# The last 128 rows of wq for ten heads of each round, laid on partitions 0 to 63 and loaded as eight shares of four rows

## The chip, the cores and the metric

One Trainium2 chip, one core, one launch. The metric is the device time of that launch in microseconds (us). The kernel before took 713.16 us (median of three runs, 712.34 to 713.28).

## The reference

Decoding of one token for a batch of four, through two equal rounds; each round is an attention block and a dense block, each with a residual sum. All arrays are float32.

```
W = 1024                      # the last 1024 of 4096 cached positions; 32 heads of 128; D = 640; Dff = 1728
q = (layernorm(x) @ wq) by heads;  k, v = the last W positions of the caches
p = softmax(q . k * 128**-0.5);  o = p . v
x = x + o @ wo                                   # attention
x = x + relu(layernorm(x) @ w1) @ w2             # dense
# both lines twice, with the same weights and caches
```

For one head this reads 640 x 128 numbers of wq, 4 x 1024 x 128 of k, as many of v, and 128 x 640 of wo: 4.85 MB. The two rounds together read 301 MB from HBM, and there is little arithmetic on each number.

## The kernel before

**The tape.** The host lays everything that belongs to one head side by side as a record of REC = 9472 columns on 128 partitions: columns 0 to 639 are wq (five blocks of 128 rows, each with 128 columns of the head), then 4096 columns of k, 4096 of v and 640 of wo. The 32 records lie one behind the other in `rec`. One partition's row of the tape is contiguous, so a load of n columns is 128 rows of 4n bytes.

**Loads.** `store` holds five records and the front of a sixth, `ring` 4320 columns more. A list `items` is written when the program is built: every load in its order, with its place in `store`, `ring` or `kept`. `pump` (line 278) takes loads from the front of that list as long as the columns they go to are free, and `done` (line 300) frees columns when their last reader has been written down. All loads are issued by SP, in the list's order; an issue waits on the chip until the last reader of its columns is through. `group` (line 210) loads five records as three transfers of some 8 MB (lists FIVE, LAST_FIVE and THREE, lines 82 to 85), `ending` cuts the last three heads finer, and the weights of the dense block (`wm`) follow.

**Work on a head.** `query` (line 385) multiplies x by the head's wq: five matmuls of 128 x 128 with four moving columns, accumulated in `misc`. `scores` makes q . k, `softmax` and `weights` the probabilities, `values` the product with v, `project` the product with wo. Engines run in the order in which the code is written (`InOrder`, line 88): head n+1's scores stand ahead of head n's values on TensorE, and head n+2's query behind them.

**Rounds.** Round 0 takes heads 0 to 31, round 1 heads 27 to 31 first, which are still in `store`, and then 0 to 26. Around the dense block of round 0 the loads are small, as `store` holds the five heads that are kept, and `ring` and what is spare carry the weights and then the front of the next heads.

Of the kernel before, what the change touches and what calls it, by code (L numbers as in the profile page):

```python
# [32 lines left out]
F32 = mybir.dt.float32  # L33
# [5 lines left out]
P = 128  # L39
B, D, H, DH, W, FF = 4, 640, 32, 128, 1024, 1728  # L40
NB = 4
FD = D // NB
KB = FD // 32
# [3 lines left out]
WQ, K, V, WO = 0, D, D + 4 * W, D + 8 * W  # L47
REC = 2 * D + 8 * W
HALF = REC // 2
VH = 2 * W  # L50

NS = 5
# [23 lines left out]
CUTS = [*range(0, K, DH), *range(K, WO, 512), *range(WO, REC + 1, FD)]  # L76
# [2 lines left out]
LATE = 6  # L79


FIVE = [REC + 6272, 2 * REC - 3072, 2 * REC - 3200]
LAST_FIVE = [REC + 4736, 2 * REC - 4736, REC, REC]
THREE = [REC + HALF, REC + HALF]
GROUPS = [{h: FIVE for h in range(0, 25, 5)}, {6: THREE, 9: FIVE, 14: FIVE, 19: LAST_FIVE}]


class InOrder:
# [18 lines left out]


@with_exitstack
def decode_kernel(ctx: ExitStack, tc: tile.TileContext, xf, rec, wm, out):  # L110
# [18 lines left out]
    rows = sb.tile([P, 2 * B], F32, name="rows")  # L129
    pick, rrow = rows[:, :B], rows[:, B:]  # L130
    mrt = sb.tile([P, B], F32, name="mrt")
    small = sb.tile([P, 14], F32, name="small")
# [41 lines left out]
    LAST = H - NS  # L174


    def home(h, r):

        if r:
            return FIRST + (h if h >= LAST else h - 6 + LAST) % NS * REC  # L180
        return (0 if h < NS else FIRST) + h % NS * REC

    items = []

    at = {("rec", 1, LAST - 1): [(KEPT, REC, "kept", 0)], ("rec", 1, 0): [(0, FIRST, "store", 0)]}
    live = []
    spare = home(H - 1, 0)
    buffers = {"store": store, "ring": ring, "kept": kept}

    def load(src, lo, hi, buf, col, parts):  # L190
        items.append((src[:, lo:hi], buf, col, hi - lo, parts))

    def place(buf, col):
        return ("store", spare + FROM + col) if buf == "spare" else (buf, col)
# [1 line left out]
    def weight(r, lo, hi, buf, col):  # L196
        buf, col = place(buf, col)
        load(wm, lo, hi, buf, col, [(("w", r), lo, hi, col)])


    def run(r, lo, hi, buf, col):
        parts = [(("rec", r, h), max(lo - h * REC, 0), min(hi - h * REC, REC), col + max(h * REC - lo, 0))
                 for h in range(lo // REC, (hi - 1) // REC + 1)]
        load(rec, lo, hi, buf, col, parts)

    def piece(r, h, lo, hi, buf="store", col=None):
        run(r, h * REC + lo, h * REC + hi, buf, home(h, r) + lo if col is None else col)


    def group(r, h, sizes):  # L210
        lo = 0
        for size in sizes:
            run(r, h * REC + lo, h * REC + lo + size, "store", home(h, r) + lo)
            lo += size

    def ending(r, hs, late):
        a, b, c = hs[-3:]
# [14 lines left out]
    for h in hs[:-3]:  # L232
        if h in GROUPS[0]:
            group(0, h, GROUPS[0][h])
        if h >= 25:
# [10 lines left out]
    new = hs[NS:]  # L246
# [8 lines left out]
    cuts = [h * REC + x for h in new[1:6] for x in CUTS]  # L255
    c, end = new[1] * REC, new[6] * REC
    for buf, lo, hi in places:
        if lo == old[1]:
            piece(1, new[0], WO, REC, buf, lo)
        elif c < end:  # L260
            cut = max(x for x in cuts if x <= min(end, c + hi - lo))
            run(1, c, cut, buf, lo)
            c = cut
    assert c == end
    for h in new[6:-3]:
        if h in GROUPS[1]:
            group(1, h, GROUPS[1][h])
        if not any(g <= h < g + sum(z) // REC for g, z in GROUPS[1].items()):
            piece(1, h, 0, REC)
    ending(1, hs, False)  # L270
    for ks in W1_SLOT:
# [1 line left out]
    n = 0  # L273
# [4 lines left out]
    def pump():  # L278

        while items:  # L280
            src, buf, col, n, parts = items[0]
# [11 lines left out]
    def cols(key, lo, n):  # L293

        for x, y, buf, col in pieces(key):
            if x <= lo and lo + n <= y:
                return buffers[buf][:, col + lo - x:col + lo - x + n]
# [84 lines left out]
    def xblock(k):  # L382
        return xT[:, 32 * k:32 * k + B]

    def query(r, h, n, first=False):
        key = ("rec", r, h)
        early = r == 1 and n < 2
        q = acc[:, 504 + 4 * n:508 + 4 * n] if early else misc[:, :B]
        for k in range(KB):
            pe.matmul(q, cols(key, WQ + k * DH, DH), xblock(k), start=(k == 0 and not early),  # L390
                      stop=(k == KB - 1), skip_group_check=True)
        done(key, WQ, K)
        if first:
            dve.tensor_copy(qT, q)
        else:
            dve.tensor_tensor(qT, q, rrow, op=OP.mult)
# [104 lines left out]
    for r in range(2):  # L501
        hs = order[r]
        late = LATE if r == 0 else 2
        center(384 * r, 128)
        query(r, hs[0], 0, True)
        if r:
            busy(192, warm)
        scores(r, hs[0], 0, True)
        softmax(0, (r, hs[1], 1))
        if r:  # L510
            unpark(2)
            unpark(3)
# [91 lines left out]
```

## Time and profile before

| what | value |
|---|---|
| three runs | 712.34, 713.16, 713.28 us |
| span of the profiled execution, first to last instruction | 710.7 us |
| HBM read over that span | 301.34 MB, 424 GB/s |
| TensorE matmul busy | 502.4 us (71%) |
| VectorE busy | 317.4 us (45%) |
| ScalarE busy | 99.6 us (14%) |
| largest wait of SP, whose waits are for room in the buffers: PE acc | 355.7 us, 33 times |

The page gives the span of the profiled execution and no time of its own beside it; what lies between the span and the median of the runs is 2.5 us. The busy shares are of the span. A DMA share is a mean over the 16 DMA engines of the core: 0.50 in a window can mean that all sixteen worked half of the time, or that eight of them had finished. Packets are counted in the window in which they start, so in a window of a microsecond or two a share can stand a little over 1.00.

### The profile page before, as it was taken

Reading aid. Unit: us, or ns where it says so; the run is one execution under the profiler, and the core shown is the slowest. Engines: PE = TensorE matmul, PEld = TensorE weight load, DVE = VectorE, ACT = ScalarE, POOL = GpSimd, SP = SyncE. Lnnn points to the kernel's source line nnn. Section 1 sums busy time; section 2 is a strip of 40 time slices with the busy share of each in tenths; the row PEclk is TensorE's granted clock in tenths of the full one; section 3 lists DMA queues with packets and bytes.
Section 4 is the critical chain, followed back from the end, with each engine's and each line's share of the span. In section 5 each row is a group of like instructions: output and inputs, shape, how many; then the busy total and the mean of one; then the engine's idle time right before and its main releaser. Section 6 shows DMA issues by size and latency. Waiting matters only on the chain.

```text
span 710.7 us, 8613 instructions
## 1 busy us (share of the span) xinstructions
PE 502.4 (71%) x3722; PEld 199.5 (28%) x3722; DVE 317.4 (45%) x645; ACT 99.6 (14%) x210; POOL 1.1 (0%) x9
## 2 busy tenths in 40 slices
PE   0675677576677686868788998756577685695985
PEld 0331322231332222333223333322222231332322
DVE  2252344253443353546541866625244253453661
ACT  0210111011010110111130421201010011011120
POOL 0000000000000000000000000000000000000000
PEclk9987787677676778788999999969687677788899
DMA  9999999999999999999999999999999999999996
GB/s 397 436 416 451 422 435 447 417 435 447 420 429 451 427 429 420 425 444 420 426 404 396 411 425 434 447 429 436 442 431 433 434 428 436 430 427 421 430 427 281
DMA packets 12741, 301.97 MB, mean 425 GB/s; under 512 B 1424, under 2 KB 1568, under 8 KB 4640
## 3 DMA queue, kind: packets, MB, share of 16 engines
q1 hardware_dynamic: 12672, 301.42, 98.9%
q8 instruction: 29, 0.48, 0.2%
q14 instruction: 8, 0.07, 0.0%
q10 hardware_dynamic: 32, 0.01, 0.0%
HBM read 301.34 MB, written 0.08 MB: 424 GB/s over the span
## 4 chain that ended last, share of the span: by engine, by line
DMA 68%; PE 25%; DVE 4%; another core or an unknown queue 1%; ACT 1%; issue 1%; SPq 0%; ACTq 0%
DMA store<-rec 60%; PE sc_ps L102 10%; PE o_ps L102 7%; DMA store<-wm 5%; PE acc L102 3%; PE misc L102 3%; DMA ring<-wm 3%; DVE scratch L102 2%; DVE o_ps L102 2%; PE t_ps L102 2%; ACT oTs L102 1%; DVE small L102 0%; ACT sc_ps L102 0%; DVE sc_ps L102 0%
## 5 line engine op out<-in xcount | busy, mean ns | idle before, releaser
L102 PE MATMUL sc_ps<-store,qT 128*4 128x512 f32 x1024 | 193.7, 852 | 37.8 <-DMA store<-rec 36.4
L102 PE MATMUL misc<-xT,store 128*128 128x4 f32 x620 | 92.8, 276 | 100.6 <-DMA store<-rec 100.0
L102 DVE TENSOR_REDUCE small<-sc_ps 128x1 f32<-128x1024 f32 x64 | 78.4, 1224 | 157.9 <-PE sc_ps L102 157.8
L102 PE MATMUL o_ps<-store,scratch 128*16 128x512 f32 x960 | 142.1, 667 | 4.6 <-DVE scratch L102 2.9
L102 PEld LDWEIGHTS misc<-xT,store 128*128 128x128 f32 x620 | 87.4, 221 | 156.2 <-DMA store<-rec 123.1
L102 ACT ACTIVATE sc_ps<-sc_ps,small 128x1024 f32<-128x1024 f32 x64 | 69.8, 1091 | 325.2 <-DVE small L102 325.2
L102 DVE STREAM_TRANSPOSE sc_ps<-sc_ps 128x1024 f32<-128x1024 f32 (+1 forms) x70 | 81.7, 1167 | 0.1
L102 PEld LDWEIGHTS sc_ps<-store,qT 128*4 128x4 f32 x1024 | 32.7, 107 | 121.2 <-issue 66.4
L102 PEld LDWEIGHTS o_ps<-store,scratch 128*16 128x16 f32 x960 | 32.3, 114 | 118.6 <-issue 100.7
L102 DVE TENSOR_TENSOR o_ps<-o_ps,of_block 128x512 f32<-128x512 f32 x62 | 43.4, 699 | 45.9 <-PE o_ps L102 45.8
L102 DVE TENSOR_TENSOR qT<-misc,rows 128x4 f32<-128x4 f32 x61 | 9.5, 156 | 112.7 <-PE misc L102 112.6
L102 PE MATMUL acc<-store,oTs 128*4 128x160 f32 x488 | 34.6, 365 | 17.1 <-ACT oTs L102 17.0
L102 DVE TENSOR_REDUCE scratch<-o_ps 128x128 f32<-128x512 f32 x62 | 42.9, 692 | 2.1
L102 ACT COPY oTs<-t_ps 128x4 f32<-128x4 f32 x59 | 9.6, 162 | 204.5 <-PE t_ps L102 204.5
L102 PE MATMUL t_ps<-rows,scratch 128*128 128x4 f32 x118 | 25.5, 286 | 11.4 <-DVE scratch L102 10.9
L102 PEld LDWEIGHTS t_ps<-rows,scratch 128*128 128x128 f32 x118 | 21.4, 226 | 17.9 <-DVE scratch L102 14.2
L102 DVE TENSOR_TENSOR scratch<-sc_ps,mrt 128x128 f32<-128x128 f32 (+1 forms) x70 | 19.6, 280 | 2.7
L102 PE MATMUL acc<-kept,small 128*1 128x328 f32 (+2 forms) x54 | 17.4, 428 | 0.0
L99 PE MATMUL acc<-scratch,ring 128*128 128x160 f32 x2 | 0.9, 540 | 22.2 <-DMA scratch<-xf 22.2
L102 DVE TENSOR_SCALAR mrt<-of_batch,small 128x4 f32<-128x4 f32 x64 | 14.7, 230 | 2.2
L102 DVE STREAM_TRANSPOSE scratch<-small 128x32 f32<-128x32 f32 x64 | 12.9, 202 | 2.4 <-ACT sc_ps L102 2.4
L102 PEld LDWEIGHTS acc<-store,oTs 128*4 128x4 f32 x488 | 6.9, 84 | 22.9 <-ACT oTs L102 21.9
(84 smaller groups left out, 123.1 us busy)
## 6 DMA issues: line engine op xcount, KB each, us to landing
store<-rec SPq DMA_DIRECT2D x14, 7872.0 KB, 28.9
store<-rec SPq DMA_DIRECT2D x7, 7936.0 KB, 30.9
store<-rec SPq DMA_DIRECT2D x4, 7104.0 KB
store<-rec SPq DMA_DIRECT2D x11, 2368.0 KB, 34.8
store<-rec SPq DMA_DIRECT2D x3, 4736.0 KB, 27.2
store<-rec SPq DMA_DIRECT2D x2, 4416.0 KB, 28.3
store<-rec SPq DMA_DIRECT2D x5, 1024.0 KB, 20.2
store<-rec SPq DMA_DIRECT2D x1, 4160.0 KB, 20.7
```

The source lines that it names most:

```text
L99: r = build(*args, **kwargs)
L102: r = build(*args, **kwargs)
```

## The change

Heads 14 to 23 of each round are "split" (SPLIT). Their records on the tape lose the 128 columns of wq's fifth block (columns 512 to 639), so `rec` is 1280 columns shorter. Those blocks go into a new input, `halves`: for each of the ten heads the block's 128 rows are laid on 64 partitions, rows 0 to 63 in 128 columns and rows 64 to 127 in the 128 columns beside them, 2560 columns in all. In HBM the 64 rows lie as two times eight shares of four rows, with a fifth row of nothing behind each share. In each round two transfers, one to partitions 0 to 31 and one to partitions 32 to 63, bring them to columns 128 to 2687 of `ring`; they stand in the list ahead of the group of head 10 (round 0) and of head 14 (round 1).

The query of a split head is four matmuls as before and then two of 64 rows, the second against `upper`, a copy of the lower half of x's fifth block on partitions 0 to 63. ScalarE makes that copy once a round, at the sixth head of the loop. The sizes in FIVE, LAST_FIVE and THREE are now written as (head, column) of each cut, at the same places.

```diff
+SPLIT = range(14, 24)
+FULL = (KB - 1) * DH
+HALVES = len(SPLIT) * 2 * DH
+HALVES_AT = 128
+HALVES_BEFORE = [10, 14]
+def size(h):
+    return REC - DH if h in SPLIT else REC
...
+    def halves_of(r):
+        parts = [(("halves", r), 0, HALVES, HALVES_AT)]
+        items.append(([(halves[q][:, :4, :HALVES], 32 * q, 32) for q in range(2)], "ring", HALVES_AT, HALVES, parts))
...
+    def group(r, h, cuts):
+        if h == HALVES_BEFORE[r]:
+            halves_of(r)
...
-            sp.dma_start(buffers[buf][:, col:col + n], src)
+            for src, row, rows in shares:
+                sp.dma_start(buffers[buf][row:row + rows, col:col + n], src)
...
-        for k in range(KB):
+        split = h in SPLIT
+        for k in range(KB - split):
             pe.matmul(q, cols(key, WQ + k * DH, DH), xblock(k), start=(k == 0 and not early),
                       stop=(k == KB - 1), skip_group_check=True)
+        if split:
+            c = (h - SPLIT[0]) * 2 * DH
+            pe.matmul(q, cols(("halves", r), c, DH, 64), xblock(KB - 1)[:64], start=False, stop=False,
+                      skip_group_check=True)
+            pe.matmul(q, cols(("halves", r), c + DH, DH, 64), upper, start=False, stop=True, skip_group_check=True)
+            done(("halves", r), c, c + 2 * DH)
...
+            if n == NS:
+                act.copy(upper, xblock(KB - 1)[64:])
...
+    halves = np.zeros((2, 8, 5, HALVES), k.dtype)
...
+            both = np.concatenate([rec[h, :64, a:b], rec[h, 64:, a:b]], 1)
+            halves[:, :, :4, c:c + 2 * DH] = both.reshape(2, 8, 4, 2 * DH)
```

SP's loads of round 0 before the change, from the second on (`store<-rec 128x15744` is a transfer of 128 rows of 15744 columns; three transfers make a group of five heads):

```order
L102 DMA store<-rec 128x15872
L102 DMA store<-rec 128x15744 x2
L102 DMA store<-rec 128x15872
L102 DMA store<-rec 128x15744 x2
L102 DMA store<-rec 128x15872
L102 DMA store<-rec 128x15744 x2
L102 DMA store<-rec 128x15872
L102 DMA store<-rec 128x15744 x2
```

The same loads now, from the same one on, as far as the group of heads 15 to 19:

```order
L132 DMA store<-rec 128x15872
L132 DMA store<-rec 128x15744 x2
L132 DMA store<-rec 128x15872
L132 DMA store<-rec 128x15744
L132 DMA ring<-halves 32x1x2560 x2
L132 DMA store<-rec 128x15744
L132 DMA store<-rec 128x15872
L132 DMA store<-rec 128x15616
L132 DMA store<-rec 128x15488
L132 DMA store<-rec 128x15616 x2
```

Two transfers of 32 rows stand ahead of the group of head 10, and from that group's last transfer on each one is shorter by 128 columns for every split head in it. In round 1 the same pair stands behind the three loads of heads 9 to 13.

TensorE before, where the query of head 14 of round 0 stands among the scores, values and products of its neighbours:

```order
L102 MATMUL sc_ps_74<-store,qT 4x512 x8
L102 MATMUL o_ps<-store,scratch 16x512 x8
L102 MATMUL misc<-xT,store 128x4 x5
L102 MATMUL t_ps<-rows,scratch 128x4
L102 MATMUL acc<-store,oTs 4x160 x4
```

TensorE now, at that head:

```order
L132 MATMUL sc_ps_75<-store,qT 4x512 x8
L132 MATMUL o_ps<-store,scratch 16x512 x8
L132 MATMUL misc<-xT,store 128x4 x4
L132 MATMUL misc<-xT,ring 128x4
L132 MATMUL misc<-upper,ring 128x4
L132 MATMUL t_ps<-rows,scratch 128x4
L132 MATMUL acc<-store,oTs 4x160 x4
```

The query of a split head reads `ring` as well as `store` and has six matmuls where there were five; nothing else changed its place on TensorE.

More of the change, by code (lines that the diff above doesn't have):

```diff
@@ L79, with on_tape, runs_of @@
 LATE = 6
-FIVE = [REC + 6272, 2 * REC - 3072, 2 * REC - 3200]
-LAST_FIVE = [REC + 4736, 2 * REC - 4736, REC, REC]
-THREE = [REC + HALF, REC + HALF]
+FIVE = [(1, 6272), (3, 3200), (5, 0)]
+LAST_FIVE = [(1, 4736), (3, 0), (4, 0), (5, 0)]
+THREE = [(1, HALF), (3, 0)]
 GROUPS = [{h: FIVE for h in range(0, 25, 5)}, {6: THREE, 9: FIVE, 14: FIVE, 19: LAST_FIVE}]
+SPLIT = range(14, 24)
[5 more added lines that the diff above has]
+    return REC - DH if h in SPLIT else REC
+BASE = [sum(size(g) for g in range(h)) for h in range(H + 1)]
+def on_tape(h, lo):
+    return BASE[h] + (lo - DH if h in SPLIT and lo >= K else lo)
+def runs_of(lo, hi):
+    found = []
+    for h in range(H):
+        for a, b in ((0, FULL), (K, REC)) if h in SPLIT else ((0, REC),):
+            at = on_tape(h, a)
+            x, y = max(lo, at), min(hi, at + b - a)
+            if x < y:
+                found.append((h, a + x - at, a + y - at, x - lo))
+    return found
 class InOrder:
@@ L109, in decode_kernel @@
 @with_exitstack
-def decode_kernel(ctx: ExitStack, tc: tile.TileContext, xf, rec, wm, out):
+def decode_kernel(ctx: ExitStack, tc: tile.TileContext, xf, rec, halves, wm, out):
     nc = tc.nc
@@ L131, in decode_kernel @@
     mrt = sb.tile([P, B], F32, name="mrt")
+    upper = sb.tile([64, B], F32, name="upper")
     small = sb.tile([P, 14], F32, name="small")
@@ L174, in decode_kernel, with start @@
     LAST = H - NS
-    def home(h, r):
+    def start(h, r):
         if r:
@@ L181, in home @@
         return (0 if h < NS else FIRST) + h % NS * REC
+    def home(h, r):
+        for g, cuts in GROUPS[r].items():
+            if g and g <= h < g + cuts[-1][0]:
+                return start(g, r) + BASE[h] - BASE[g]
+        return start(h, r)
     items = []
@@ L201, in run @@
     def run(r, lo, hi, buf, col):
-        parts = [(("rec", r, h), max(lo - h * REC, 0), min(hi - h * REC, REC), col + max(h * REC - lo, 0))
-                 for h in range(lo // REC, (hi - 1) // REC + 1)]
-        load(rec, lo, hi, buf, col, parts)
+        load(rec, lo, hi, buf, col, [(("rec", r, h), a, b, col + at) for h, a, b, at in runs_of(lo, hi)])
     def piece(r, h, lo, hi, buf="store", col=None):
[L207 to L214, printed above, removed]
+        assert h not in SPLIT
+        run(r, BASE[h] + lo, BASE[h] + hi, buf, home(h, r) + lo if col is None else col)
+    def group(r, h, cuts):
+        if h == HALVES_BEFORE[r]:
+            halves_of(r)
+        lo = BASE[h]
+        for n, at in cuts:
+            hi = on_tape(h + n, at)
+            run(r, lo, hi, "store", home(h, r) + lo - BASE[h])
+            lo = hi
     def ending(r, hs, late):
@@ L254, in decode_kernel @@
     places += [("store", 0, FIRST), ("store", old[4] + FROM, old[4] + REC), ("ring", 0, RING)]
-    cuts = [h * REC + x for h in new[1:6] for x in CUTS]
-    c, end = new[1] * REC, new[6] * REC
+    cuts = [BASE[h] + x for h in new[1:6] for x in CUTS]
+    c, end = BASE[new[1]], BASE[new[6]]
     for buf, lo, hi in places:
@@ L267, in decode_kernel @@
             group(1, h, GROUPS[1][h])
-        if not any(g <= h < g + sum(z) // REC for g, z in GROUPS[1].items()):
+        if not any(g <= h < g + z[-1][0] for g, z in GROUPS[1].items()):
             piece(1, h, 0, REC)
@@ L280, in pump @@
         while items:
-            src, buf, col, n, parts = items[0]
+            shares, buf, col, n, parts = items[0]
             if any(b == buf and x < col + n and col < y for b, x, y in live):
                 return
-            sp.dma_start(buffers[buf][:, col:col + n], src)
+            for src, row, rows in shares:
+                sp.dma_start(buffers[buf][row:row + rows, col:col + n], src)
             live.append((buf, col, col + n))
@@ L291, in pieces, with cols @@
         return at[key if key in at else (key[0], 0) + key[2:]]
-    def cols(key, lo, n):
+    def cols(key, lo, n, rows=P):
         for x, y, buf, col in pieces(key):
             if x <= lo and lo + n <= y:
-                return buffers[buf][:, col + lo - x:col + lo - x + n]
+                return buffers[buf][:rows, col + lo - x:col + lo - x + n]
         raise KeyError((key, lo, n))
@@ L581 @@
     rec = np.empty((H, P, REC), k.dtype)
+    flat = np.empty((P, BASE[H]), k.dtype)
+    halves = np.zeros((2, 8, 5, HALVES), k.dtype)
     rec[:, :, WQ:K] = block_rows(np.asarray(A_wq)).reshape(KB, P, H, DH).transpose(2, 1, 0, 3).reshape(H, P, D)
@@ L585 @@
     rec[:, :, WO:] = np.asarray(A_wo).reshape(H, DH, D)
+    for h in range(H):
+        a, b = (FULL, K) if h in SPLIT else (K, K)
+        flat[:, BASE[h]:BASE[h + 1]] = np.concatenate([rec[h, :, :a], rec[h, :, b:]], 1)
+        if h in SPLIT:
+            c = (h - SPLIT[0]) * 2 * DH
+            both = np.concatenate([rec[h, :64, a:b], rec[h, 64:, a:b]], 1)
+            halves[:, :, :4, c:c + 2 * DH] = both.reshape(2, 8, 4, 2 * DH)
     w2 = np.asarray(B_w2)
@@ L591 @@
         "xf": x.reshape(B, NB, FD).transpose(1, 0, 2).reshape(NB * B, FD),
-        "rec": rec.transpose(1, 0, 2).reshape(P, H * REC),
+        "rec": flat,
+        "halves": halves,
         "wm": np.concatenate([block_rows(np.asarray(B_w1)).transpose(1, 0, 2).reshape(P, KB * FF), *tiles], 1),
```

2 lines of the change are left out of this document (1 added, 1 removed).

## The prediction

> **What bounds the kernel now.** I read the page's slices, queues and chain first.
>
> ```profile
> span 710.7 us, 8613 instructions
> PE 502.4 (71%) x3722; PEld 199.5 (28%) x3722; DVE 317.4 (45%) x645; ACT 99.6 (14%) x210; POOL 1.1 (0%) x9
> DMA  9999999999999999999999999999999999999996
> q1 hardware_dynamic: 12672, 301.42, 98.9%
> q8 instruction: 29, 0.48, 0.2%
> q14 instruction: 8, 0.07, 0.0%
> DMA 68%; PE 25%; DVE 4%; another core or an unknown queue 1%; ACT 1%; issue 1%; SPq 0%; ACTq 0%
> ```
>
> The DMA engines are busy from the first slice to the last, SP's queue alone fills 98.9% of them, and 68% of the chain that ended last is loads. The kernel is as long as its loads. Two small queues share the engines with it: 29 packets that fetch instructions on q8 and 8 on q14.
>
> The change neither adds nor saves bytes. [...] So the question is whether the sixteen engines end together. No view numbers them, but the last microseconds, in windows of half a microsecond, show how many still work (last two columns: mean share of the sixteen, GB/s):
>
> ```profile
> 702.00:702.50 0.50, 0.50 (x24) 0.42 (x14) 0.00 (x0) 0.00 (x0) 0.00 (x0) 1.00 0.98 410
> 702.50:703.00 0.50, 0.48 (x12) 0.10 (x2) 0.00 (x0) 0.00 (x0) 0.00 (x0) 1.00 0.91 379
> 703.00:703.50 0.50, 0.00 (x0) 0.00 (x0) 0.00 (x0) 0.00 (x0) 0.00 (x0) 1.00 0.74 307
> 703.50:704.00 0.50, 0.00 (x0) 0.00 (x0) 0.00 (x0) 0.00 (x0) 0.00 (x0) 1.00 0.64 261
> 704.00:704.50 0.50, 0.00 (x0) 0.00 (x0) 0.00 (x0) 0.00 (x0) 0.00 (x0) 1.00 0.54 220
> 704.50:705.00 0.50, 0.13 (x4) 0.11 (x8) 0.00 (x0) 0.00 (x0) 0.00 (x0) 1.00 0.39 159
> 705.00:705.50 0.50, 0.50 (x20) 0.40 (x16) 0.00 (x0) 0.00 (x0) 0.00 (x0) 1.00 0.42 169
> 705.50:706.00 0.50, 0.50 (x24) 0.39 (x20) 0.00 (x0) 0.00 (x0) 0.00 (x0) 1.00 0.42 140
> 706.00:706.50 0.50, 0.50 (x19) 0.35 (x14) 0.00 (x0) 0.00 (x0) 0.00 (x0) 1.00 0.17 67
> 706.50:707.00 0.50, 0.50 (x20) 0.34 (x10) 0.00 (x0) 0.00 (x0) 0.00 (x0) 1.00 0.04 15
> ```
>
> Sixteen times the share is the number at work: 15.7, 14.6, 11.8, 10.2, 8.6, 6.2, 6.7, 6.7, 2.7, 0.6. Nine engines end between 702.5 and 704.7, none in the next half microsecond, and the other seven between some 705.3 and 706.8. The half-microseconds times the shares add up to 2.6, so the mean engine ends at 704.6 and the last 2.2 us later. Perfect balance behind the last point at which all wait could gain 2.2 us there, no more.
>
> What delays the late ones? All carry the same rows of the tape, so the fetches do. A window of one microsecond around one fetch of each kind gives its time as a share of sixteen engines; the windows 405 to 707 us and 0 to 355 us give their numbers:
>
> ```profile
> q8 instruction: 1, 0.02, 5.8%
> q14 instruction: 1, 0.01, 1.9%
> ...
> q8 instruction: 14, 0.23, 0.3%
> q14 instruction: 3, 0.02, 0.0%
> ...
> q8 instruction: 12, 0.20, 0.2%
> q14 instruction: 3, 0.02, 0.0%
> ```
>
> A q8 fetch takes 0.058 x 16 = 0.93 us, a q14 fetch 0.30 us. Spread over all sixteen, 14 fetches from 405 us on would set engines apart by one fetch at most. Two clusters with middles 2.5 us apart (703.6 and 706.1) say that they fall on half the engines: 14 on eight is 1.75 each, which asks 1.4 us a fetch, 0.93 and some 0.5 lost beside it by the interrupted packet (an estimate). By the same half microsecond a q14 fetch costs 0.3 to 0.8.
>
> **The change part by part.** *Bytes.* From 560 to 600 us the engines run undisturbed:
>
> ```profile
> 560.00:600.00 40.00, 27.61 (x190) 11.44 (x194) 16.19 (x33) 4.26 (x10) 0.00 (x0) 0.76 1.00 435
> ```
>
> 435 / 16 = 27.2 GB/s an engine. The tape loses 10 heads x 128 columns x 4 bytes = 5,120 bytes on each of 128 partitions a round; an engine that serves eight of them is relieved of 40,960 bytes, 1.51 us. The new transfers bring eight shares of four rows of 10,240 bytes, twice: 81,920 bytes on each of eight engines, 3.01 us (at the 25.1 GB/s an engine of the window 705.0 to 705.5, where rows are 5 KB and less, 3.26). So in each round eight engines get 1.5 to 1.75 us more, I take 1.55, and eight get 1.51 less. [...]
>
> [...] No row of before has such a transfer; were all sixteen used, the sum of this part would be nothing.
>
> *Who is late.* If only relieved engines were late, they would end at 706.8 - 2 x 1.51 = 703.8 and the loaded ones, all among the early nine, at 704.7 + 1.55 to 3.1 = 706.3 to 707.8: from 0.5 us better to 1.0 worse, as the move is larger than the gap. But seven are late and nine early, so with eight in a half at least one of the half with the q8 fetches is early, and for each further one an engine of the other half is late. [...] One engine that takes two of the three q14 fetches behind 405 us is 0.6 to 1.6 us behind its neighbours, and from 703.6 that reaches the gap. I take it that one loaded engine ends at 705.3, the early edge of the late cluster.
>
> *What carries from round 0 to the end.* Between the rounds the loads are small and wait for room:
>
> ```profile
> 355.00:405.00 50.00, 42.08 (x410) 15.42 (x406) 22.96 (x58) 12.12 (x23) 0.00 (x0) 1.00 1.01 401
> ...
> 325.79 33.97 DMA store<-rec
> 359.77 8.88 DMA ring<-wm
> ...
> 369.66 6.76 DMA ring<-wm
> ```
>
> 401 GB/s against 435 over 50 us is 3.9 us of lost transfer a mean engine, some of it small rows (at 25.1 GB/s, 402, all of it). So between nothing and 3.9 us of waiting lies here, and early engines wait longest. But each of these loads is waited for until its last engine has landed, and the next is issued after that: a laggard drags the lull with it. So of the 1.55 us that the loaded laggard gets in round 0, between 0 and 1.55 reaches the end; I take 1.4, near the upper end, because the chain is made of load waits until here and so follows the last engine. It ends at 705.3 + 1.4 + 1.55 = 708.25, **1.4 us** behind the 706.8 of now.
>
> *TensorE.* Each split head gets one matmul and one weight load more, and two of the six have 64 rows.
>
> ```profile
> L102 PE MATMUL misc<-xT,store 128*128 128x4 f32 x620 | 92.8, 276 | 100.6 <-DMA store<-rec 100.0 <-DVE xT L102 0.3
> PE misc L102 <- DMA store<-rec: 21.8, 5, 6.4
> PE misc L102 <- DMA store<-rec: 20.7, 5, 6.5
> ```
>
> A matmul of a query is two instructions (620 = 2 x 310), so at most 0.55 us a head and 5.5 us for the ten heads of a round. The cover is in TensorE's waits from 150 to 270 us and from 530 to 660 us, which hold the split heads of the two rounds: it waits for loads ahead of queries 21.8 and 20.7 us, five times each. It costs nothing. Without that cover it would be 5.5 us a round. The 64-row form is not in the trace; between nothing and a full matmul it hides the same way.
>
> *ScalarE's copy.* The nearest row is the 128 x 4 copy:
>
> ```profile
> 439.59 0.16 ACT L102 COPY oTs<-t_ps 128x4 f32<-128x4 f32 x1 [1.21 <-PE t_ps L102]
> ```
>
> 0.16 us twice, ahead of an exponential for which ScalarE waits anyway (1.21 us idle before this copy). Nothing, or 0.3 us if that idle time were gone.
>
> *SP.* Two issues more a round, at some 0.35 us each, ahead of an issue that waits for room; the columns of `ring` they fill were left by the opening or by head 5 long before. No new wait falls on what stands behind them. [...]
>
> **Sum.** 0 (TensorE, ScalarE, SP) + 1.4: the span goes from 710.7 to 712.1 us. The profiled execution lies 2.5 us under the median of the runs, which I keep: **714.6 us**.
>
> **The rivals.**
>
> *The late half is the relieved half and no loaded engine is late.* For it speak the two clusters. As above, the lull eats much of round 0's share: 706.3 to 706.6, so 712.5 to 713.0, take 712.7. Chance 0.22.
>
> *Faster.* The same, and the lull eats all of round 0's load on the early engines while the relieved ones keep both of theirs; the last loaded engine that matters is then one near the middle of the early cluster, 703.6 + 1.55 = 705.2, and the gain is 1.6 us: 711.5. It decides from the point where the laggards of the stretch up to 360 us are all relieved ones, as then the lull itself comes up to 1.5 us earlier, too. Against it: q14's fetches. Chance 0.16.
>
> *The late half is the loaded half.* Then both loads fall on the last engine: 2 x 1.5 to 1.75, 716.2 to 716.7. Nothing in the views excludes it, since none numbers the engines. Chance 0.07.
>
> *The relieved engines stand idle while the shares load.* The 2 x 327,680 bytes of a round last 3.0 us on eight engines instead of 1.5 on sixteen; if the next 8 MB transfer doesn't follow at once on the other eight, every round loses 1.5 us: 713.2 + 3.0 = 716.2. It decides where the next issue comes later than the shares' end. Against it stand the full slices: the queue always holds a transfer more. Chance 0.05. [...]
>
> *The shares do not do what they say* and go over all sixteen engines: only some 16 packets more, 713.2. Chance 0.03.
>
> **How the numbers follow.** The forecast has the rest, 0.47; with all of the laggard's first load kept it is 714.8, with none 713.2. A measurement here can tell about 0.2%, 1.4 us, from no change, and the forecast lies on that bound; I put 0.33 of it beyond and 0.14 within. Slower: 0.33 + 0.07 + 0.05 = 0.45. Within: 0.14 + 0.22 + 0.03 = 0.39. Faster: 0.16. The range leaves out the far half of the faster case and what lies beyond the two cases at 716.2: 711.6 to 716.2.
>
> **What would show it.** In the last windows the stair should lose its two clusters: more engines early (the relieved at 702 to 705), and a thin tail of one or two (share 0.06 to 0.12) up to 708. SP's queue should show two transfers of 320 KB to `ring` a round, TensorE's waits under the query should shrink by about 0.5 us a head, and the lull should begin 0 to 1 us later. I am wrong if the last engine ends by 705.5 (no loaded laggard), or if the tail is eight engines wide (the loaded half was the late one).

## The result, and the profile after

The changed kernel takes **718.32 us** (median of six runs, 716.64 to 719.59) against 712.76 for the kernel before beside it: a ratio of 1.0076, 95% interval 1.006 to 1.0092, or 5.4 us slower (4.3 to 6.6). The forecast was 714.6 with a range up to 716.2: the sign was right, the time lies outside.

The page of the changed kernel, the lines that answer to those of before (span; TensorE's busy time; the DMA engines' share in 40 slices; packets, MB and share of time of each queue; the chain that ended last):

```profile
span 716.9 us, 8704 instructions
PE 503.7 (70%) x3762; PEld 208.5 (29%) x3762; DVE 318.5 (44%) x645; ACT 99.9 (14%) x212; POOL 1.1 (0%) x9
DMA  9999999999999999999999999999999999999995
q1 hardware_dynamic: 12832, 301.42, 98.5%
q8 instruction: 29, 0.48, 0.3%
q14 instruction: 8, 0.07, 0.0%
DMA 73%; PE 22%; DVE 2%; ACT 1%; issue 1%; SPq 0%; ACTq 0%
```

The bytes are those of before, the queue is nearly as full as before, and yet it is later. 98.5% of 716.9 us is 706.1 us of packet time an engine, against 98.9% of 710.7, 702.9, before. So about half of the 6.2 us is engines that stand idle at some time, and the other half is the same bytes moved in more time.

Where the engines end, by windows of a microsecond (last two columns: share of the sixteen, GB/s):

```profile
705.00:706.00 1.00, 0.71 (x4) 0.08 (x1) 0.93 (x4) 0.00 (x0) 0.00 (x0) 1.00 1.00 417
706.00:707.00 1.00, 0.00 (x0) 0.00 (x0) 0.22 (x2) 0.00 (x0) 0.00 (x0) 1.00 0.82 339
707.00:708.00 1.00, 0.58 (x20) 0.51 (x24) 0.00 (x0) 0.00 (x0) 0.00 (x0) 1.00 0.78 320
708.00:709.00 1.00, 1.00 (x34) 0.71 (x24) 0.00 (x0) 0.00 (x0) 0.00 (x0) 1.00 0.67 252
709.00:710.00 1.00, 0.22 (x4) 0.00 (x0) 0.00 (x0) 0.00 (x0) 0.00 (x0) 1.00 0.25 102
710.00:711.00 1.00, 0.00 (x0) 0.00 (x0) 0.00 (x0) 0.00 (x0) 0.00 (x0) 1.00 0.15 61
711.00:712.00 1.00, 0.82 (x25) 0.64 (x29) 0.00 (x0) 0.00 (x0) 0.00 (x0) 1.00 0.10 38
712.00:713.00 1.00, 1.00 (x36) 0.74 (x28) 0.00 (x0) 0.00 (x0) 0.00 (x0) 1.00 0.07 26
```

The shares from 705 on add up to 3.8, so the mean engine ends at 708.8, where it was 704.6; the last one ends near 713, where it was 706.8. The thin tail that was forecast is there (0.15, 0.10, 0.07: one or two engines), but up to 713 and not to 708. What was not forecast is that **all** engines are later: the share is 1.00 up to 706, and the mean end is 4.2 us later. The lull between the rounds begins later, too: by the trace's packet records (start, duration and bytes of each packet) the transfer that had landed at 354.5 us lands 2.4 us later, where 0 to 1 was forecast.

The remaining terms (the two groups of matmuls of 64 rows, with busy time and mean ns of one; TensorE's waits under the query from 150 to 270 and from 530 to 660 us; the copy to `upper`; the new transfers):

```profile
L132 PE MATMUL misc<-xT,ring 64*128 64x4 f32 x40 | 8.8, 289 | 0.0
L132 PE MATMUL misc<-upper,ring 64*128 64x4 f32 x40 | 8.4, 280 | 0.0
...
PE misc L132 <- DMA store<-rec: 19.8, 5, 6.1
...
PE misc L132 <- DMA store<-rec: 20.5, 5, 8.7
...
L132 ACT COPY upper<-xT x2: 192/192/192, 101.1 to 435.0; 64x4 f32<-64x4 f32 x2
...
ring<-halves SPq DMA_DIRECT2D x4, 320.0 KB
```

Four transfers of 320 KB, a copy of 0.19 us twice, matmuls of 0.28 us: these are as forecast. The waits under the query went from 21.8 to 19.8 and from 20.7 to 20.5.

### The profile page after: what moved, and what is told of

It reads as the page before. It is cut to its first block, busy times and chain, and to the rows that moved or that the text cites. A ratio compares the mean times of both kernels' runs of the same rounds, so it can differ in the third digit from the quotient of the medians.

```text
span 716.9 us, 8704 instructions
## 1 busy us (share of the span) xinstructions
PE 503.7 (70%) x3762; PEld 208.5 (29%) x3762; DVE 318.5 (44%) x645; ACT 99.9 (14%) x212; POOL 1.1 (0%) x9
## 3 DMA queue, kind: packets, MB, share of 16 engines
q1 hardware_dynamic: 12832, 301.42, 98.5%
## 4 chain that ended last, share of the span: by engine, by line
DMA 73%; PE 22%; DVE 2%; ACT 1%; issue 1%; SPq 0%; ACTq 0%
DMA store<-rec 67%; PE sc_ps L132 8%; PE o_ps L132 6%; DMA store<-wm 4%; PE misc L132 4%; PE acc L132 3%; DMA ring<-wm 2%; PE t_ps L132 1%; DVE scratch L132 1%; DVE o_ps L132 1%; ACT oTs L132 1%; DVE small L132 0%; ACT sc_ps L132 0%; DVE sc_ps L132 0%; ACTq L132 0%
## 5 line engine op out<-in xcount | busy, mean ns | idle before, releaser
L132 PE MATMUL sc_ps<-store,qT 128*4 128x512 f32 x1024 | 183.4, 814 | 48.1 <-DMA store<-rec 46.7
L132 PE MATMUL misc<-xT,store 128*128 128x4 f32 x580 | 88.2, 278 | 99.9 <-DMA store<-rec 99.6
L132 PE MATMUL o_ps<-store,scratch 128*16 128x512 f32 x960 | 144.8, 681 | 3.1 <-DVE scratch L132 1.8
L132 PEld LDWEIGHTS misc<-xT,store 128*128 128x128 f32 x580 | 82.8, 222 | 156.8 <-DMA store<-rec 121.3
```

The source lines that it names most:

```text
L132: r = build(*args, **kwargs)
```

## The experiments

Eighteen more kernels were run, each beside the kernel before. The table gives the byte of a partition at which `store` begins, which turned out to matter; the other columns are the median and the ratio to before with its 95% interval. The kernel before, beside them, had medians from 712.07 to 712.76 us, so differences between runs are taken from the ratios.

| run | `store` at | us | ratio |
|---|---|---|---|
| the changed kernel | 3104 | 718.32 | 1.0076 (1.006 to 1.0092) |
| e1_sixteen | 3104 | 724.77 | 1.0175 (1.0151 to 1.0199) |
| e2_five_heads | 3104 | 717.0 | 1.0061 (1.004 to 1.0083) |
| e3_three_parts | 3104 | 717.92 | 1.0083 (1.0066 to 1.01) |
| e4_tape_whole | 3104 | 720.59 | 1.0114 (1.0099 to 1.0129) |
| e5_all_partitions | 3104 | 716.02 | 1.0045 (1.003 to 1.0061) |
| e6_sixth_matmul | 3072 | 712.25 | 0.9996 (0.9986 to 1.0005) |
| e7_relief_only | 3104 | 712.53 | 1.0003 (0.9989 to 1.0016) |
| e8_upper | 3104 | 726.67 | 1.0189 (1.0166 to 1.0212) |
| e9_before_shifted | 3104 | 715.82 | 1.0058 (1.0045 to 1.0071) |
| e10_after_aligned | 3136 | 717.14 | 1.0075 (1.0061 to 1.0088) |
| e11_all_partitions_aligned | 3136 | 714.97 | 1.0043 (1.0031 to 1.0056) |
| e12_relief_aligned | 3136 | 711.99 | 1.0 (0.9989 to 1.0011) |
| f1_upper_last | 3072 | 714.75 | 1.0032 (1.0018 to 1.0047) |
| f2_all_partitions_upper_last | 3072 | 712.45 | 1.0001 (0.9991 to 1.0012) |
| f3_relief_upper_last | 3072 | 709.43 | 0.9957 (0.9944 to 0.9969) |
| f4_before_at_2816 | 2816 | 712.14 | 0.9997 (0.9986 to 1.0009) |
| f5_five_heads_upper_last | 3072 | 712.41 | 0.9999 (0.9988 to 1.001) |
| f6_before_at_2944 | 2944 | 714.98 | 1.0037 (1.0023 to 1.005) |

### Is it the uneven load?

**e1_sixteen**: the halves as 32 rows of a plain array, which sixteen engines share, to the same 64 partitions.

```diff
-        items.append(([(halves[q][:, :4, :HALVES], 32 * q, 32) for q in range(2)], "ring", HALVES_AT, HALVES, parts))
+        items.append(([(halves[q], 32 * q, 32) for q in range(2)], "ring", HALVES_AT, HALVES, parts))
-    halves = np.zeros((2, 8, 5, HALVES), k.dtype)
+    halves = np.zeros((2, 32, HALVES), k.dtype)
...
```

> The same 64-row blocks, places, order and matmuls as in the changed kernel, but the source has no fifth rows, so that each transfer of 32 rows can be split over sixteen engines, two rows each. If the cost of the change is the load on eight engines: back to the kernel before, 712.3 to 713.7 us, and the last windows show the stair of before. If it is the two added transfers, the matmuls of 64 rows or the copy on ScalarE: still 717 to 719 us.

724.77 us: slower than the change by 6 us, which neither theory had expected. Its queue shows that sixteen engines took part:

```profile
q1 hardware_dynamic: 12864, 301.42, 98.8%
```

That is 192 packets more than before, for 128 rows and, by the records, 64 packets of 4 bytes, 16 for each of the four transfers. Before has 1,408 of them for its 88 loads, 16 each, so they are taken as one for each engine that has a part in a transfer: by that count sixteen engines. The change has 160 more, 128 rows and 32 of 4 bytes, 8 a transfer: by that count eight engines. The windows in which the pair of round 1 loads, of e1 and then of the changed kernel (share, GB/s):

```profile
546.00:548.00 2.00, 0.00 (x0) 0.00 (x0) 0.00 (x0) 0.00 (x0) 0.00 (x0) 0.68 1.20 423
548.00:550.00 2.00, 0.00 (x0) 0.00 (x0) 0.00 (x0) 0.00 (x0) 0.00 (x0) 0.50 0.84 196
550.00:552.00 2.00, 0.00 (x0) 0.00 (x0) 0.00 (x0) 0.00 (x0) 0.00 (x0) 0.50 1.66 314
552.00:554.00 2.00, 0.00 (x0) 0.00 (x0) 0.00 (x0) 0.00 (x0) 0.00 (x0) 0.50 0.79 170
```

```profile
546.00:548.00 2.00, 1.25 (x8) 0.33 (x12) 0.00 (x0) 0.00 (x0) 0.00 (x0) 0.50 1.19 510
548.00:550.00 2.00, 2.00 (x12) 0.34 (x7) 1.22 (x1) 0.06 (x1) 0.00 (x0) 0.50 1.11 480
```

A window counts a packet whole where it starts, so single windows swing; the durations in the packet records are surer. In e1 a row of the halves (10,240 bytes) takes 743 ns in the median of round 1, in the change 389, and rows of the next 8 MB transfer that run at the same time take 3.8 us in place of 2.3. With each packet's bytes spread over its own duration, e1 moves 190 to 227 GB/s from 550 to 556 us, with all sixteen engines busy. In the change eight engines write to the same partitions while the others are at the next 8 MB transfer, and from 540 to 552 us the sixteen move 421 to 433 GB/s: next to nothing is lost. So sixteen engines did not bring the shares to these 64 partitions more cheaply than eight: the rate fell to 190 to 227 GB/s, in which rows of the next transfer are counted, too.

**e2_five_heads** halves the load (heads 14 to 18 alone), **e3_three_parts** brings the halves in parts, each ahead of the group that is relieved, and **e4_tape_whole** loads the halves but leaves the tape whole, so that no engine is relieved.

```diff
-SPLIT = range(14, 24)
+SPLIT = range(14, 19)
```

```diff
-HALVES_BEFORE = [10, 14]
+HALVES_BEFORE = [{10: (14, 15), 15: (15, 20), 20: (20, 24)}, {14: (14, 19), 19: (19, 24)}]
...
-        if h == HALVES_BEFORE[r]:
-            halves_of(r)
+        if h in HALVES_BEFORE[r]:
+            halves_of(r, *HALVES_BEFORE[r][h])
```

```diff
-    return REC - DH if h in SPLIT else REC
+    return REC
...
```

> Heads 14 to 18 alone are split, so every share and the relief are half as large. If the load on eight engines is the cost and it is in proportion: half of the 5.6 us, 715 to 716 us. If there is a slack that the first part of the load uses up: under 714 us. If the number of transfers costs: over 717 us.

> The halves come in parts, each ahead of the group of heads that it belongs to (three pairs of transfers in round 0, two in round 1), so that the load on the eight engines and the relief of all sixteen come together. If the cost comes from 3 us of load that stand ahead of their relief (the last engine lags most at that time, TensorE and the next issue wait for it, the early engines run dry): 714.5 to 716.5 us. If only the sum of the bytes on the late engines counts: unchanged, 717.5 to 719 us.

> The halves are loaded and used as in the changed kernel, but the tape keeps the 128 columns of every split head, which nobody reads: the load on eight engines without the relief. Every engine gets 40,960 bytes a round more than in the changed kernel, 1.5 us. If the relief works in full on the engines that are late: 3.0 us more, 721.0 to 721.8 us. If it comes too late to be of use: 718 to 719.5 us.

Half of the load costs 0.61%, all of it 0.76%: the loss isn't proportional to it. Load and relief side by side (e3) give 1.0083, within the noise the change's own: that the load comes ahead of its relief isn't the loss. Without any relief (e4) the median rises by 2.3 us, between the two cases that were expected. So the loss does not go with the uneven load, and something else must cost, too.

**e8_upper** sends the eight shares to partitions 64 to 127.

```diff
-        items.append(([(halves[q][:, :4, :HALVES], 32 * q, 32) for q in range(2)], "ring", HALVES_AT, HALVES, parts))
+        items.append(([(halves[q][:, :4, :HALVES], 64 + 32 * q, 32) for q in range(2)], "ring", HALVES_AT, HALVES, parts))
...
```

> The same transfers of eight shares, but to partitions 64 to 127; the halves of x's fifth block change places accordingly. If the eight shares go to the engines of the upper half, these are then the loaded ones: if most of the late engines are there, over 720 us; if most of the late are in the lower half, under 716 us. [...]

```profile
548.00:550.00 2.00, 0.00 (x0) 0.00 (x0) 0.00 (x0) 0.00 (x0) 0.00 (x0) 0.50 0.59 129
550.00:552.00 2.00, 0.00 (x0) 0.00 (x0) 0.00 (x0) 0.00 (x0) 0.00 (x0) 0.50 1.05 217
```

726.67 us, over 720, and the same picture as e1: 129 and 217 GB/s, and a row of the halves takes 809 ns. The queue has the 12,832 packets of the change, so by the count above eight engines carry the shares here, too; in the change, to partitions 0 to 63, a row takes 389 ns and the sixteen keep 421 to 433 GB/s. So what the shares cost depends on the half of the partitions that they go to. Which eight engines carry them, and why the half matters, is not shown: no record names an engine or a partition.

### Taking the change apart

**e5_all_partitions** loads the same columns evenly, to all 128 partitions in two transfers a round ahead of the same groups, with the tape as short as the change's and six matmuls of full height; **e6_sixth_matmul** is the kernel before with the first query matmul done twice for heads 14 to 23; **e7_relief_only** has the short tape and loads no halves: its matmuls of 64 rows read what lies in `ring`, and the fifth blocks are left out of its result.

```diff
-        items.append(([(halves[q][:, :4, :HALVES], 32 * q, 32) for q in range(2)], "ring", HALVES_AT, HALVES, parts))
+        for q in range(2):
+            load(halves, q * n, q * n + n, "ring", HALVES_AT + q * n, [(("halves", r), q * n, q * n + n, HALVES_AT + q * n)])
...
```

```diff
-        for k in range(KB):
+        for k in ([0] if 14 <= h < 24 else []) + list(range(KB)):
```

```diff
-        if h == HALVES_BEFORE[r]:
-            halves_of(r)
...
```

> [...] The query of a split head has six matmuls (one of the first block is made twice; the result stays). If the uneven load is the cost: as the kernel before, 712.0 to 713.5 us. If the place of the blocks in the order, the two transfers or the sixth matmul cost: 714 us or more.

> The kernel before with one thing added: for heads 14 to 23 of each round the query's first matmul is made twice, so that these queries have six. If TensorE's waits for loads cover it: 712.0 to 713.3 us. If the next issue hangs on TensorE behind a landing at some places (0.5 to 0.8 us seen at one of them in the changed kernel): 713.5 to 715 us.

> The tape is shortened as in the changed kernel, but the halves are not loaded; the two matmuls of 64 rows read what lies in the ring, so the fifth block of wq of ten heads is left out of the result. The relief alone: every engine has 40,960 bytes a round less. If bytes count in full: 3.0 us under the kernel before, 709.0 to 710.0 us. If the matmuls of 64 rows, the copy on ScalarE and the other cuts cost something of their own, it shows here as less than that.

The sixth matmul is free (0.9996). But an even load costs 3.2 us (1.0045), and 3 us fewer bytes on every engine gain nothing (1.0003). Both point the same way: **a common 3 us is lost whatever is loaded**. The packet records show where. Most rows of the ordinary loads, in all kernels with the tile `upper` ahead of `store`, take a few ns more than in the kernel before. The median ns of a row, by its size, of runs shown here and below:

```
bytes in a row           6912   8192  18944  63488   store at
before                    262    309    705   2342   3072 = 12 x 256
f1_upper_last             262    309    705   2342   3072
f4_before_at_2816         262    309    705   2342   2816 = 11 x 256
changed kernel            266    313    708   2346   3104 = 12.125 x 256
e9_before_shifted         266    313    708   2346   3104
e10_after_aligned         265    312    707   2345   3136 = 12.25 x 256
f6_before_at_2944         265    312    707   2345   2944 = 11.5 x 256
```

Some 3 ns a row, whether it is 7 KB or 63 KB. What these kernels share is the place of the buffers (the program's allocation names each tile's first byte): `upper` is allocated between `mrt` and `small`, takes 32 bytes of each partition, and moves `small`, `store`, `kept` and `ring` on by as much. (`kept` and `ring` begin at multiples of 256 bytes wherever `store` does; no run moves one of the three alone.)

### The start of `store`

**e9_before_shifted** is the kernel before with an unused tile in that place; **e10**, **e11** and **e12** are the change, e5 and e7 with `upper` made 64 bytes wide.

```diff
     mrt = sb.tile([P, B], F32, name="mrt")
+    shift = sb.tile([64, B], F32, name="shift")
...
+    dve.memset(shift, 0.0)
```

```diff
-    upper = sb.tile([64, B], F32, name="upper")
+    upper = sb.tile([64, 4 * B], F32, name="upper")[:, :B]
```

> The kernel before with one unused tile of 16 bytes a partition where the change has its tile upper; every load is that of before. In the changed kernel and in all experiments that have upper, the tiles behind it (small, store, kept, ring) begin 32 bytes later, so store begins at byte 3104 of a partition (48.5 times 64) in place of 3072 (48 times 64), and every row of the tape's loads took some 3 to 10 ns longer. Theory A, the 32 bytes cost each row that time: 715 to 716 us, with rows of 63 KB at about 2346 to 2353 ns in place of 2342. Rival B, the rows are slower because of the extra input in the memory or of the changed tape: 712.3, as the kernel before.

> The changed kernel, with upper given 64 bytes a partition (16 of them used), so that store begins at byte 3136, 49 times 64; nothing else differs. Theory A (the 32 bytes): the common 3 us go and only the uneven load is left, 714.5 to 715.5 us, near the 714.6 that was forecast from the loads alone. Rival B: 718, as the changed kernel.

> The balanced kernel (the block's rows loaded to all partitions, in two transfers, the tape as short as in the change), with upper given 64 bytes. Its even load cost 3.7 us with store at byte 3104. Theory A: 712 to 713, as the kernel before. Rival B: 716, as without the 64 bytes.

> The kernel that leaves the fifth block of wq of ten heads of each round unloaded (its queries read what lies in ring), with upper given 64 bytes. It loads 3.0 us less on every engine and gained nothing with store at byte 3104. Theory A: the gain shows, 709 to 710 us. Rival B: 712.5, as without the 64 bytes; then the end isn't set by how much the queues move.

e9 settles that the shift alone costs: 1.0058 (1.0045 to 1.0071), 4.1 us, with not one load changed. Its page, and a window of the smaller rows (last column GB/s) of the kernel before, of e9 and of f1 (below):

```profile
span 713.8 us, 8614 instructions
q1 hardware_dynamic: 12672, 301.42, 98.8%
```

```profile
684.00:700.00 16.00, 13.68 (x110) 3.95 (x109) 8.62 (x26) 3.07 (x6) 0.00 (x0) 1.00 1.02 432
```

```profile
684.00:700.00 16.00, 13.79 (x121) 4.59 (x124) 10.03 (x27) 3.24 (x7) 0.00 (x0) 1.00 1.01 422
```

```profile
684.00:700.00 16.00, 13.79 (x124) 4.32 (x127) 10.02 (x27) 3.24 (x7) 0.00 (x0) 1.00 1.01 430
```

98.8% of 713.8 is 705.2 us of packets an engine, 2.3 more than before (a tenth of a per cent is 0.7 us); the packet records give 2.4, which is 704 rows of 3.4 ns. The rest of the 3.1 us by which this span is longer is idle time of the engines, 0.7 us, more than half of it between 355 and 405 us. Where rows are short the engines move 422 GB/s in place of 432. But 64 bytes didn't mend it (e10 to e12 are where they were): a multiple of 64 isn't enough. Theory A stood in its cause and fell in its measure.

**f1**, **f2**, **f3** and **f5** are the change, e5, e7 and e2 with `upper` behind `ring`, so that everything else stands where it stood before. **f4** and **f6** are the kernel before with small tiles moved behind `ring`, so that `store` begins at 2816 (a multiple of 256, not of 512) and at 2944 (a multiple of 128).

```diff
-    upper = sb.tile([64, B], F32, name="upper")
...
     ring = sb.tile([P, RING], F32, name="ring")
+    upper = sb.tile([64, B], F32, name="upper")
```

> The changed kernel with upper allocated behind ring instead of ahead of store, so that small, store, kept and ring stand at the bytes of the kernel before (store at 3072, 12 times 256); nothing else differs. Shifting these tiles by 32 bytes in the kernel before cost 4.2 us (712.17 to 715.82, with the ratio 1.0058), and 64 bytes in the changed kernel left it at 717.1. Theory A, the start of store must be a multiple of 256 bytes (or of more): the rows are as fast as before and only the uneven load is left, 713.5 to 715 us, about what was forecast. Rival B, the shift isn't what slows the changed kernel: 717 to 718.

> The balanced kernel (the fifth blocks loaded to all partitions in two transfers, as short a tape as the change's) with upper behind ring, store at byte 3072. With store at 3104 and 3136 it took 716.0 and 715.0. If the start of store was the whole of its cost: 712 to 713, as the kernel before; if the two transfers, the short tape or the copy to upper cost something of their own: 713.5 or more.

> The kernel that leaves the fifth block of wq of ten heads of each round unloaded (its queries read what lies in ring), with upper allocated behind ring, so that store begins at byte 3072. Theory A: its rows are as fast as before and the 3.0 us of fewer bytes on every engine show at the end, 709 to 709.7 us. Rival B: 712, as with store at 3104 and 3136; then the end isn't set by how much the queues move.

> The kernel before with its small tiles (oTs to small) behind ring and 64 unused bytes, so that store begins at byte 2816, 11 times 256 but not a multiple of 512; every load is that of before. If a multiple of 256 is what the rows need: 712.3, as before. If it has to be a multiple of 512 (3072 is 6 times 512): 715 to 716, as with 32 bytes more.

> The change for the five heads 14 to 18 alone (half of its uneven load), with upper behind ring, store at byte 3072. Its cost with store at 3104 was 4.3 us. Theory A, the bytes of the start cost some 3.7 us and the uneven load the rest: 712.3 to 713.5, between the kernel before and the change with upper last. Rival B: 717.

> The kernel before with its tiles rows, mrt and small behind ring, so that store begins at byte 2944, 23 times 128 but not a multiple of 256; every load is that of before. If a start must be a multiple of 256: 715 to 716, as at byte 3104. If 128 is enough (64, at 3136, was not): 712.3.

All six came out as theory A has it with 256 bytes for its measure: 2816 and 3072 are fast, 2944, 3104 and 3136 slow. The even load costs nothing any more (1.0001), 3 us fewer bytes gain 3.1 us (0.9957), and **the change without the shifted buffers takes 714.75 us**, 0.32% more than before. Between the two places the ratio differs by 0.44% for the change, 0.44% for the even load and 0.46% for the relief: some 3.1 to 3.3 us of the change's 5.4 are the start of `store`, and 2.3 (1.3 to 3.3) are the uneven load. The split is no finer than that: half of the load gives 0.62% (e2 against f5) for the start, f6 0.37%, and the intervals of most ratios are 0.1 to 0.15% to either side.

How that load costs its 2.3 us, by the ends of the engines in f1 and then in f5, which has half of it:

```profile
702.00:703.00 1.00, 0.51 (x3) 0.00 (x0) 0.90 (x5) 0.00 (x0) 0.00 (x0) 1.00 1.00 426
703.00:704.00 1.00, 0.13 (x4) 0.14 (x8) 0.05 (x1) 0.00 (x0) 0.00 (x0) 1.00 0.92 389
704.00:705.00 1.00, 1.00 (x36) 0.81 (x32) 0.00 (x0) 0.00 (x0) 0.00 (x0) 1.00 0.81 341
705.00:706.00 1.00, 0.67 (x17) 0.26 (x8) 0.00 (x0) 0.00 (x0) 0.00 (x0) 1.00 0.85 344
706.00:707.00 1.00, 0.00 (x0) 0.00 (x0) 0.00 (x0) 0.00 (x0) 0.00 (x0) 1.00 0.53 215
707.00:708.00 1.00, 0.42 (x14) 0.33 (x18) 0.00 (x0) 0.00 (x0) 0.00 (x0) 1.00 0.28 113
708.00:709.00 1.00, 1.00 (x38) 0.78 (x28) 0.00 (x0) 0.00 (x0) 0.00 (x0) 1.00 0.17 69
709.00:710.00 1.00, 1.00 (x28) 0.58 (x26) 0.00 (x0) 0.00 (x0) 0.00 (x0) 1.00 0.06 23
```

```profile
702.00:703.00 1.00, 1.00 (x23) 0.61 (x25) 0.90 (x5) 0.00 (x0) 0.00 (x0) 1.00 1.00 428
703.00:704.00 1.00, 1.00 (x33) 0.79 (x24) 0.15 (x1) 0.00 (x0) 0.00 (x0) 1.00 0.94 397
704.00:705.00 1.00, 0.24 (x4) 0.00 (x0) 0.00 (x0) 0.00 (x0) 0.00 (x0) 1.00 0.91 376
705.00:706.00 1.00, 0.15 (x7) 0.13 (x11) 0.00 (x0) 0.00 (x0) 0.00 (x0) 1.00 0.67 277
706.00:707.00 1.00, 1.00 (x36) 0.80 (x32) 0.00 (x0) 0.00 (x0) 0.00 (x0) 1.00 0.57 219
707.00:708.00 1.00, 1.00 (x32) 0.69 (x24) 0.00 (x0) 0.00 (x0) 0.00 (x0) 1.00 0.14 46
```

In f1 the shares add up to 4.6 from 702 on: the mean engine ends at 706.6, 2.0 later than before, and the last at 709.5, 2.7 later. In f5 the mean engine ends at 706.2 and the last at 707.8, 1.0 later than before; but this execution took 713.29 us, 0.9 more than f5's median, which is that of before.

Which engines are late can be read from the packet records: a packet begins 3 to 4 ns ahead of the end of the one before it on the same engine, so most engines can be followed back from their last row. In f1 the eight that end last, from 706.8 to 709.5, are the eight that carried the shares of round 1, and the others end by 706.5. So the whole loaded half is late, and the thin tail is its slowest one or two. In f5, with half of the load, the two kinds are mixed: loaded ones end from 705.5 to 707.8, and others as late as 707.2.

Where the mean engine's 2 us come from, as no bytes were added, is less clear. By the packet records of f1 the last engine of a transfer is 2.9 us later behind the halves of round 0, 1.5 later by 357 us as the relief comes, and the mean of all engines 0.8; on the far side of the dense block, at 440 us, both are 2.1 later. It looks as if the engines waited there for the last one and took over its lateness. But in f5 the last engine is 1.0 us earlier than before at 354 us, and at 440 us both are 1.8 to 1.9 later all the same; so it isn't shown that a late engine causes what is lost around the dense block.

None of the kernels that compute everything beats the kernel before: e6, f2, f4 and f5 equal it.

## Why the prediction was wrong, and where it was right

- **"The change neither adds nor saves bytes ... So the question is whether the sixteen engines end together."** This is the step that failed. The sum has terms for bytes, fetches and waits, and none for the rate of the loads that were not touched; `upper` stood in it only as ScalarE's copy. The tile moved every buffer by 32 bytes, most rows then took some 3 ns more, and that cost 3.1 us of the 5.4 (the change against f1; 4.1 in e9, where it stands alone). None of the rivals had it.
- **The uneven load, +1.4 us**: not told apart from what was measured, at its low end. That eight engines would take the shares, 81,920 bytes each, was shown by no row of before; the 160 packets more of the change count eight engines. Alone, in f1, it is 2.3 us (1.3 to 3.3); on top of the shifted buffers (the change against e9) it is 1.3. That f1 takes 714.75 us where 714.6 was forecast is luck: the forecast stands on 713.16, the kernel before beside f1 took 712.52. The 2.5 us between span and time were also partly chance, as in the executions behind it they are 1.7 (the change's profiled one: 718.59 and 716.9). The bytes term was right: 3.1 us gained in f3 where 2 x 1.51 was worked out.
- **"What carries from round 0 to the end"**: a laggard 1.5 us ahead of the last engine was to get 1.4 here and 1.55 in round 1, 1.4 in all. In f1's records the last engine is 2.1 us later behind the dense block, more than the 1.55 that was the upper bound, and the mean engine as much; round 1 adds 0.6. That is 2.7 in this execution. The carry was mis-sized, and it was not of one engine: all were later there. Why is open, as f5 shows the same without a late engine ahead of it.
- **One loaded laggard among the late engines**: the thin tail came, in the change up to 713 and in f1 up to 709.5, but this is not how it came about. In f1 all eight loaded engines end behind the others. The fetches were priced right: in the records of the kernel before a q8 fetch takes 0.93 us and the row behind it some 0.49 more, 1.43 in the median of 28, where 1.4 was estimated. They do fall on eight engines in turn, as was inferred (twelve fetches of f1 up to 341 us); but two of these eight carry the shares, so a loaded laggard needs no q14 fetch.
- **TensorE's sixth matmul, nothing**: right (e6, 0.9996), with the cover that was named. The waits under the query shrank by 2.0 and 0.2 us where about 0.5 us a head was expected; with loads that themselves come later this tells little.
- **ScalarE's copy and SP, nothing**: f2 has the copy to `upper` and the additional issues, and stands at 1.0001.
- **The rivals.** The relieved engines did not stand idle while the halves of round 1 loaded: all sixteen are busy, and the 421 to 433 GB/s above are near the rate around them. The shares went to eight engines, not sixteen, as the 160 packets more show (e1, with sixteen, has 192 more). Two of the eight engines that have the fetches are in the loaded half; so a late half made by the fetches, as the prediction has it, is neither all loaded nor all relieved. In f1 the loaded half is the late one, but at a cost of 2.3 us and not of the 3.0 to 3.5 of that rival. A faster kernel is excluded by f1. In the first rival 706.3 is 0.5 us under 706.8, so its times begin at 712.7 and not at 712.5; nothing hangs on it.

## What to carry to other kernels

A small new tile can move all that is allocated behind it: here `upper`, 32 bytes of a partition, moved `store` from 3072 to 3104, and such a move alone cost 4.1 us in e9. Ask where the big DMA destinations begin before and after, and put small tiles behind them or fill them up (here, so that the destinations begin at a multiple of 256 bytes: the kernel before ran at 0.9997 with `store` at 2816 in place of 3072, at 1.0037 with 2944 and at 1.0058 with 3104). When an edit that moves no bytes costs time, take it apart with a control that has the edit's set-up and none of its work: e9 told in one run what the eight runs ahead of it had not. And in this kernel a load that is uneven over engines was free where the loaded engines end among the others (f5, 0.9999), and cost 2.3 us where they end behind them (f1).

## What the hardware showed that was not expected

**The start of a row in SBUF.** With `store` at a multiple of 256 bytes the median row of a size takes the same time to the nanosecond (262 ns for 6912 bytes); 32, 64 or 128 bytes beside it, 2 to 4 ns more, the same for 7 KB and for 63 KB. So it is a price per row, and 704 rows an engine make 2.4 us of it; the rest of the 3.1 to 4.1 us is not in the packets' durations. In the execution of e9 that was profiled it is idle time, 0.7 us, and why the engines are idle longer is not shown. In the first 60 us, and for most of the rows between the rounds, the rows of e9 were not slower, and why not is open too. In e9 not one load was changed and only the side that is written was moved. By the table the runs show 3 to 4 ns at 32 bytes beside the multiple of 256, 2 to 3 at 64 and 2 to 3 at 128: not growing with the distance. What makes a row longer there is not shown.

**Engines and partitions.** With sixteen engines on 64 partitions (e1) all are busy and yet move 190 to 227 GB/s, half of the 433 around it: there a busy DMA share was not a rate.

**Fetches of instructions.** In the kernel before a fetch of 16 KB cost its DMA engine 1.43 us (median of 28), 0.49 of it on the row behind the fetch. That kernel's engines end up to 4 us apart (702.8 to 706.8); that the fetches make this difference is inferred, from two clusters of ends and from f1's fetches, which fall on eight engines.
